# Block 0's plain float32 second products cut from eight feature chunks to four, and its share of the attention steps moved one or two slots later

## The chip, the cores and the metric

The kernel runs on one core of a Trainium2 chip. The metric is the device time of one execution in microseconds (us), from the first to the last instruction of the slowest core (there is only one). A time is the median over runs. The profile comes from one execution that was recorded by the hardware profiler.

## What is computed

```python
# 1. attention in chunks of 32 queries over a window of 16 + 32 + 8 keys and 8 memory keys
scores = (q_c @ k_full.T) / 8
a = exp(scores - max) / (sum + 1e-9)
out_c = a @ v_full
# 2. x = attention output as 3072 tokens x 512
h = x @ w_in                      # 512 -> 2048
y = (h * cos(h)) @ w_out          # 2048 -> 512
# 3. three products, maximum, one product
z = max(y @ w1, y @ w2, y @ w3)   # 512 -> 768
result = z @ w_out2               # 768 -> 512
```

All of it is float32 work. The weights arrive as 64-bit floats and are turned into 32-bit floats on the chip.

## The kernel before

The 3072 tokens go in six blocks of 512 (`j`). In part 2 each block is taken in 16 chunks of 128 features (`f`); one chunk of one block is a **slot**, so there are 96 slots in a row. Block 0 is slots 0 to 15. In slot `s` three things are written into the program:

- `p1(j, f)`: the first product of chunk `f`. Its result `h` goes to a PSUM buffer. From chunk 2 on, block 0 uses the two buffers of `ps_h` in turn, so the product of chunk f writes into the buffer that chunk f-2 used.
- `chain(j, f)`: h times cos(h). In block 0 it is a copy to integers on ScalarE (L429), a subtraction on VectorE (L430), Sin and Square on ScalarE (L433, L434) and a product with `h` on VectorE (L438 or L443), which is the last to read `h`. Its result is `g`.
- `p2`: the second product, two slots behind (`LOOK = 2`), into four PSUM accumulators.

A product is normally made of three matmuls of the type float32r (L392), of a high part and a low part of each operand: high by high, high by low, low by high. So `g` and the weights have to be split: a copy on ScalarE gives the high part (L446 for `g`, L206 for weights), and a subtraction on GpSimd (L447 for `g`; L207 for weights of the first product) or VectorE (L207 for weights of the second product) gives the low part. In block 0, for chunks below `PLAIN`, the second product is instead one matmul of plain float32 (L389; the trace counts two instructions for each), which needs no split of `g`, and the split of that chunk's weight is put off: `split_out` does it from slot `SPLIT0` on, a fixed fraction of a chunk in each slot (`SPLITS`), so that block 1 has it.

In block 0 the engines beside TensorE also decode the weights: per slot one chunk of either weight is loaded, its top bits are taken (L181 on ScalarE, L183 on GpSimd), it is put together (L198 on VectorE), and chunks decoded one slot earlier are split.

Beside all this, block 0 computes the attention of block 1, in four parts `d` of 128 queries. The tables `FIRST` (block 0), `SECOND` (block 1) and `STEADY` say in which slot each step of it stands: `S` scores on TensorE (L246) into the two buffers of `ps_a`, then a sum with the mask and a maximum on VectorE (L263, L269) and a subtraction on GpSimd (L270); `E` Exp on ScalarE for two parts at a time (L274, with a load of ScalarE's function table before it and one back for Sin behind it); `N` the norm (VectorE L279 to L281, GpSimd L282); `T` a transpose on VectorE (L286) and a write to memory; `L` or `l` the three transfers back (`pt`, one buffer; `l` stands behind the `V` before it); `V` the product with v on TensorE (L305), the copy of its result to `x` on ScalarE (L307) and the low part on VectorE (L308). Block 1's first product, in slot 16, reads `x` of all four parts.

The order on each engine is that of the program as the scheduler put it. TensorE's order is pinned throughout, all engines' orders only for the first six slots; an engine takes its instructions strictly in order. All transfers are issued by one queue (SyncE). Parts 3 and the preparation of its weights follow later and are not touched.

Of the kernel before, what the change touches and what calls it, by code (L numbers as in the profile page):

```python
# [46 lines left out]

FIRST = {2: "S0", 3: "S1", 4: "S2", 5: "S3 E01", 6: "E23 N0", 7: "T0 N1", 8: "L0 T1 N2", 9: "V0 l1", 10: "V1 T2 N3", 11: "L2 T3", 12: "V2 l3", 14: "V3"}  # L50
SECOND = {0: "S0", 1: "S1", 2: "E01 S2", 3: "N0 S3", 4: "T0", 5: "E23 N1 L0 S4", 6: "V0 T1", 7: "L1 N2", 8: "S5 T2 N3", 9: "V1 E45", 10: "L2 S6 T3", 11: "V2", 12: "L3 S7", 13: "V3", 14: "E67"}
STEADY = {1: "N0", 2: "T0 N1", 3: "L0", 4: "S4", 5: "V0 T1 N2", 6: "L1", 7: "S5", 8: "V1 T2 N3", 9: "L2 E45", 10: "S6 T3", 11: "V2 l3", 12: "S7", 13: "V3", 14: "E67"}

# [16 lines left out]

PLAIN, SPLIT0, SPLITS = 8, 12, (0.5, 0.75)
INV2PI = 1.0 / (2.0 * math.pi)


# [1 line left out]
def attn_moe_kernel(ctx, tc, qT, kT, vw, w_in, w_out, w3, w2o, out):  # L78
# [141 lines left out]
    def a_load_qk(d):  # L220
        if d >= ND:
            return
        if d < DB:
            q = wp.tile([128, 1024], F32, tag="w", name="q")[:, :2 * 4 * QU].rearrange("p (t h c) -> p t h c", t=2, h=4)
            k = wp.tile([128, 1024], F32, tag="w", name="k")[:, :4 * KD].rearrange("p (h c) -> p h c", h=4)
            live[0] += 2
        else:
            q = t2.tile([128, 2, 4, QU], F32, tag="q", name="q")
            k = t2.tile([128, 4, KD], F32, tag="k", name="k")
        SP.dma_start(out=q, in_=qT[d])  # L230
        SP.dma_start(out=k, in_=kT[d])
        qk[d] = (q, k)
# [16 lines left out]
    def a_scores(d):  # L249
        ss[d] = [ps_a.tile([128, 4, KU], F32, tag="a", name="s") for _ in range(2)]  # L250
        for t in range(2):
            a_s(d, t, ss[d][t], True, keep)
# [4 lines left out]
    def a_add(d):  # L257
        m = sm[d] = t2.tile([128, KB * H * 32], F32, tag="sm", name="sm", bufs=4)
        m = by_key(d)
        p = ss.pop(d)  # L260
        for t in range(2):
            mask = maskb[:, variant(d, t), None, :].to_broadcast([128, 4, KU])
            DVE.tensor_tensor(m[:, 4 * t:4 * t + 4], p[t].rearrange("p h (b k) -> p h b k", b=KB),  # L263
                              mask.rearrange("p h (b k) -> p h b k", b=KB), op=ALU.add)

    def a_max(d):
        m = by_key(d)
        mx = t2.tile([128, H], F32, tag="mx", name="mx")
        DVE.tensor_reduce(mx, m, axis=AX.XY, op=ALU.max)  # L269
        POOL.tensor_tensor(m, m, mx[:, :, None, None].to_broadcast([128, H, KB, 32]), op=ALU.subtract)  # L270

    def a_exp(j, ds):
        for d in (DB * j + i for i in ds):
            keep(ACT.activation(out=sm[d], in_=sm[d], func=AF.Exp, scale=0.125))  # L274

    def a_norm(d):
        m = by_key(d)
        r = t2.tile([128, H], F32, tag="rs", name="rs")
        DVE.tensor_reduce(r, m, axis=AX.XY, op=ALU.add)  # L279
        DVE.tensor_scalar(r, r, 1.0e-9, None, op0=ALU.add)  # L280
        DVE.reciprocal(r, r)  # L281
        POOL.tensor_tensor(m, m, r[:, :, None, None].to_broadcast([128, H, KB, 32]), op=ALU.mult)  # L282
# [6 lines left out]
    def a_l(d):  # L289
        pt[d] = t2.tile([128, 4, H, 32], F32, tag="pt", name="pt", bufs=1)  # L290
        for b in range(KB):
            keep(SP.dma_start(out=pt[d][32 * b:32 * b + 32].rearrange("p a h q -> p a (h q)"),
                              in_=ptd[d % 2][:, 256 * b:256 * b + 256].rearrange("(a p) e -> p a e", a=4)))
# [100 lines left out]
    def p1(j, f):  # L394
        if f % 2 and (done[0] or j == 0 and f == 1):
            h = ps_a.tile([128, N], F32, tag="a", name="h")
        else:
            h = ps_h.tile([128, N], F32, tag="h", name="h")
        w, x = wA_in[f], xT[j]
        for k in range(4):  # L400
            products(h, w, k, [x[:, i, k, :] for i in range(2)], k == 0, k == 3)
        live[0] -= j == NBLK - 1
        hq[j, f] = h
# [4 lines left out]
    def wa_fetch(j, f):  # L408
        if j and f >= RES:
            w = w_tile([128, 2, 512], "wa")  # L410
            SP.dma_start(out=w.rearrange("p a c -> p (a c)").bitcast(F32), in_=wad[f])
            wA_out[f] = (w[:, 0, :], w[:, 1, :])
# [53 lines left out]
    def p2(j, f):  # L466
        g, w = g_t.pop((j, f)), wA_out[f]
        if f == 0:
            acc[j] = [ps_acc.tile([128, N], F32, tag=f"acc{m}", name=f"acc{m}") for m in range(4)]
        for m in range(4):  # L470
            products(acc[j][m], w, m, [g[:, i, :] for i in range(2 if j or f >= PLAIN else 1)], f == 0, f == FA - 1)
        live[0] -= f >= RES or j == NBLK - 1
        if f == FA - 1:
            for m in range(4):
                if m < 3:
                    t = tr.tile([128, N], F32, tag="r", name="x2")
                elif done[0]:
                    t = tmp["pool"].tile([128, N], F32, tag="xo", name="x2", bufs=6)
                else:
                    t = t2.tile([128, N], F32, tag="x2", name="x2", bufs=1)  # L480
                if m % 2 == 0:
                    ACT.activation(out=t, in_=acc[j][m], func=AF.Copy, scale=1.0 if j else -2.0)
                elif j:
                    DVE.tensor_copy(t, acc[j][m])
                else:
                    DVE.tensor_scalar(t, acc[j][m], -2.0, None, op0=ALU.mult)
                SP.dma_start(out=x2d[j][:, m, :], in_=t)
# [57 lines left out]
    def flush():  # L545
        while later:
            out, in_ = later.pop(0)
            keep(SP.dma_start(out=out, in_=in_))
# [61 lines left out]
    def prep_go(upto):  # L610
        while prep_n[0] < min(upto, len(prep)):
            prep[prep_n[0]]()
            prep_n[0] += 1
# [366 lines left out]
    def slot(s):  # L980
        j, f = slots[s]
        plan = {0: FIRST, 1: SECOND}.get(j, STEADY)
        todo = plan.get(f, "").split() if j < NBLK - 1 else []
        base = DB * (j + 1)

        ready = dec.nb
        if s < turn:
            dec.begin(RATE)
        if s < FA:
            parts = int(max(0, s - SPLIT0 + 1) * SPLITS[0])  # L990
        else:
            parts = int((FA - SPLIT0) * SPLITS[0] + (s - FA + 1) * SPLITS[1])

        def fill(where):
            if s < 2:
                if where == "z":
                    dec.split_in(ready)
                    dec.bits()
                    dec.load()
                return  # L1000
            if where == "z":
                prep_go(int(sum(i % FA not in QUIET for i in range(PREP0, s)) * PREPS))
            if s >= turn:
                if where == "z":
                    for fn in early.get(s - total, ()):
                        fn()
                return
            if where == "a0":
                dec.split_in(ready)
            elif where == "a1":  # L1010
                dec.split_out(parts)
            elif where == "d0":
                dec.bits(1)
            elif where == "z":
                dec.bits()
                dec.exp(dec.nb + 2)
                dec.load()

        for op in todo:
            if op[0] == "L" and base + int(op[1:]) < ND:  # L1020
                a_l(base + int(op[1:]))
        while wf[0] < min(s + (3 if s >= turn else 2), total):
            wa_fetch(*slots[wf[0]])
            wf[0] += 1
        flush()
        p1(j, f)
        chain(j, f, fill, [base + int(op[1:]) for op in todo if op[0] == "T" and base + int(op[1:]) < ND])

        def do2():
            while n2[0] <= s - LOOK:  # L1030
                p2(*slots[n2[0]])
                n2[0] += 1

        for op in todo:
            d = base + int(op[1:2])
            if d >= ND:
                continue
            if op[0] == "S":
                do2()
                a_scores(d)  # L1040
                a_add(d)
                a_load_qk(d + 2)
                a_max(d)
            elif op[0] == "E":
                a_exp(j + 1, map(int, op[1:]))
            elif op[0] == "N":
                a_norm(d)
            elif op[0] == "l":
                a_l(d)
            elif op[0] == "V":  # L1050
                do2()
                a_v(d)
                a_load_v(d + 2)
        do2()
# [117 lines left out]
```

## Time and profile before

| | |
|---|---|
| median of 3 runs | 965.54 us (965.42 to 965.87) |
| the profiled execution, its own time | 967.37 us |
| its span, first to last instruction | 965.5 us |
| TensorE busy | 954.3 us (99%) |
| VectorE, ScalarE, GpSimd busy | 613.6, 461.7, 413.1 us |

How to read it: the profile names engines PE (TensorE matmuls), PEld (its weight loads), DVE (VectorE), ACT (ScalarE), POOL (GpSimd) and SP (SyncE). L392 is line 392 of the kernel. In a timeline each row gives the start, the duration, the engine, the line, the operation, the result and operands, and in brackets the time that the engine had stood idle and what ended that. Matmuls overlap, so the time one takes is read from one start to the next.

### The profile page before, as it was taken

To read this page: it belongs to the slowest core of one execution; us is meant where nothing else is said; L and a number is where in the kernel's file an instruction comes from. 1 tells how busy PE (TensorE), PEld (TensorE's weight loads), DVE (VectorE), ACT (ScalarE), POOL (GpSimd) and SP (SyncE) were. 2 spreads that over 40 slices of the span, in tenths; PEclk is the share of its full clock that TensorE was granted. 3 is DMA by queue.
4 is the path that set the end of the run, shared out by engine and by line. 5 is a ranking of instruction groups with operands and counts; after the bars stand their busy time and mean duration, and the time that the engine had idled before them with its cause. 6 is when DMAs were issued, how large, how long until landed. Compare 5 with 4: busy or idle time off the path is not lost.

```text
span 965.5 us, 14586 instructions
## 1 busy us (share of the span) xinstructions
PE 954.3 (99%) x5372; PEld 770.0 (80%) x5373; DVE 613.6 (64%) x923; ACT 461.7 (48%) x801; POOL 413.1 (43%) x333
## 2 busy tenths in 40 slices
PE   8999999999999999999999999999999999999998
PEld 5666788888888888888888888888888888888886
DVE  7688856655667656765646475644784657945565
ACT  6667645555445554564545545523363332723333
POOL 3566535534345445445434355435501545025520
PEclk9999999999999999999999999999999999999999
DMA  9986633563557855775477739695568647595502
GB/s 289 337 306 198 224 126 103 160 197 142 192 198 221 252 196 174 226 227 186 147 216 247 241 113 323 226 319 164 174 229 330 243 135 230 202 390 172 193 23 88
DMA packets 75911, 201.75 MB, mean 209 GB/s; under 512 B 8256, under 2 KB 21056, under 8 KB 75840
## 3 DMA queue, kind: packets, MB, share of 16 engines
q1 hardware_dynamic: 75552, 200.56, 62.2%
q8 instruction: 43, 0.70, 0.3%
q10 hardware_dynamic: 288, 0.26, 0.1%
q14 instruction: 28, 0.23, 0.1%
HBM read 154.13 MB, written 46.66 MB: 208 GB/s over the span
## 4 chain that ended last, share of the span: by engine, by line
PE 93%; DMA 3%; DVE 2%; ACT 1%; issue 1%; SPq 0%; POOL 0%; DVEq 0%; ACTq 0%
PE hb L734 27%; PE h L392 26%; PE acc L392 23%; PE hb L861 9%; PE s L246 3%; PE acc L389 3%; PE s L305 2%; DMA v<-in_vw_dram 1%; DMA k<-in_kT_dram 1%; DMA pt<-ptd 1%; ACT ki L455 0%; DVE ki L453 0%; DVE ki L452 0%; DVE ki L457 0%; PE s L356 0%
## 5 line engine op out<-in xcount | busy, mean ns | idle before, releaser
L392 PE MATMUL h<-x,w 128*128 128x512 f32 x1152 | 283.9, 395 | 0.0
L392 PEld LDWEIGHTS h<-x,w 128*128 128x128 f32 x1152 | 213.1, 188 | 48.7 <-issue 1.4
L462 POOL TENSOR_TENSOR g<-ki,g 128x512 fp32r<-128x512 f32 x80 | 108.5, 1356 | 213.5 <-ACT g L461 187.4
L734 PE MATMUL hb<-x,wq 128*128 128x512 f32 x648 | 155.7, 389 | 0.0
L734 PEld LDWEIGHTS hb<-x,wq 128*128 128x128 f32 x648 | 121.6, 188 | 25.3
L392 PE MATMUL acc<-g,w 128*128 128x512 f32 x576 | 138.3, 389 | 0.0
L392 PEld LDWEIGHTS acc<-g,w 128*128 128x128 f32 x576 | 108.1, 188 | 22.5
L734 PE MATMUL hb<-xo,wq 128*128 128x512 f32 x486 | 119.1, 389 | 0.0
L392 PE MATMUL acc<-g,wa 128*128 128x512 f32 x480 | 115.6, 389 | 0.2 <-POOL g L462 0.2
L455 ACT ACTIVATE ki<-ki,pio 128x512 f32<-128x512 f32 x80 | 58.1, 726 | 108.1 <-DVE ki L453 107.9
L734 PEld LDWEIGHTS hb<-xo,wq 128*128 128x128 f32 x486 | 91.2, 188 | 18.9
L392 PEld LDWEIGHTS acc<-g,wa 128*128 128x128 f32 x480 | 90.0, 188 | 19.3 <-POOL g L462 0.6
L760 POOL TENSOR_TENSOR p<-p,p 128x512 f32<-128x512 f32 x27 | 38.4, 1421 | 144.7 <-ACT p L757 144.7
L452 DVE SCALAR_TENSOR_TENSOR ki<-h,ki 128x512 f32<-128x512 f32 x80 | 54.9, 686 | 68.5 <-ACT ki L450 68.5
L457 DVE TENSOR_TENSOR ki<-h,ki 128x512 f32<-128x512 f32 x80 | 55.2, 690 | 55.0 <-ACT ki L455 55.0
L861 PE MATMUL hb<-g,wo 128*128 128x512 f32 x378 | 86.2, 389 | 0.0
L861 PEld LDWEIGHTS hb<-g,wo 128*128 128x128 f32 x378 | 70.9, 188 | 14.7
L461 ACT ACTIVATE g<-ki 128x512 fp32r<-128x512 f32 x80 | 50.6, 633 | 59.0 <-DVE ki L457 58.9
L450 ACT ACTIVATE ki<-h 128x512 int32<-128x512 f32 x80 | 47.2, 590 | 58.6 <-PE h L392 52.1
L760 DVE TENSOR_TENSOR a<-a,hb 128x512 f32<-128x512 f32 x27 | 18.5, 684 | 72.1 <-PE hb L734 72.1
L553 DVE TENSOR_TENSOR wq<-raw,wq 128x512 fp32r<-128x512 f32 x36 | 44.1, 1244 | 24.6 <-ACT wq L552 24.5
L198 DVE SCALAR_TENSOR_TENSOR raw<-raw,top 128x512 int32<-128x512 int32 x48 | 45.9, 956 | 16.3 <-ACT top L181 16.2
(126 smaller groups left out, 1213.3 us busy)
## 6 DMA issues: line engine op xcount, KB each, us to landing
wq<-wd SPq DMA_DIRECT2D x81, 512.0 KB, 6.5
wa<-wad SPq DMA_DIRECT2D x40, 512.0 KB, 6.0
wo<-wod SPq DMA_DIRECT2D x30, 512.0 KB, 4.5
wd<-wq SPq DMA_DIRECT2D x27, 512.0 KB, 2.9
v<-in_vw_dram SPq DMA_DIRECT2D x24, 384.0 KB, 5.8
raw<-in_w_dram SPq DMA_DIRECT2D x18, 511.8 KB, 5.3
raw<-in_w_in_dram SPq DMA_DIRECT2D x16, 511.8 KB, 10.3
raw<-in_w_out_dram SPq DMA_DIRECT2D x16, 511.8 KB, 10.0
```

The costliest lines, as they stand in the source:

```text
L198: keep(DVE.scalar_tensor_tensor(o, z, 13, top[key], op0=ALU.logical_shift_right, op1=ALU.bitwise_or))
L392: PE.matmul(o, lhsT=w[a][:, sl], rhs=x[b], start=first and n == 0, stop=last and n == 2)
L450: row(ACT.activation(out=ki, in_=h, func=AF.Copy, scale=INV2PI, bias=0.25))
L452: row(DVE.scalar_tensor_tensor(c, h, INV2PI, ki, op0=ALU.mult, op1=ALU.subtract))
L455: row(ACT.activation(out=c, in_=c, func=AF.Sin, scale=2 * math.pi, bias=pio2))
L457: row(DVE.tensor_tensor(c, h, c, op=ALU.mult))
L461: row(ACT.activation(out=g[:, 0, :], in_=c, func=AF.Copy))
L462: row(POOL.tensor_tensor(g[:, 1, :], c, g[:, 0, :].bitcast(F32), op=ALU.subtract))
L553: keep(eng.tensor_tensor(w[:, 1, :], src, w[:, 0, :].bitcast(F32), op=ALU.subtract))
L734: keep(PE.matmul(o, lhsT=w[:, a, 256 * half + 128 * c:256 * half + 128 * c + 128], rhs=x[c][:, b, :], start=first and n == 0, stop=n == 5, ...
L760: keep(eng.tensor_tensor(o, a, b, op=op))
L861: keep(PE.matmul(bk[i][b], lhsT=w[:, s, x, 128 * i:128 * i + 128], rhs=g[:, y, :], start=b not in seen and c == 0 and m == 0, stop=c == 2 ...
```

## The change

```diff
-FIRST = {2: "S0", 3: "S1", 4: "S2", 5: "S3 E01", 6: "E23 N0", 7: "T0 N1", 8: "L0 T1 N2", 9: "V0 l1", 10: "V1 T2 N3", 11: "L2 T3", 12: "V2 l3", 14: "V3"}
+FIRST = {3: "S0", 4: "S1", 5: "S2", 6: "S3 E01", 7: "E23 N0", 8: "T0 N1", 9: "L0 T1 N2", 11: "V0 l1", 12: "V1 T2 N3", 13: "L2 T3", 14: "v2 l3", 15: "v3"}
...
-PLAIN, SPLIT0, SPLITS = 8, 12, (0.5, 0.75)
+PLAIN, SPLIT0, SPLITS = 4, 14, (0.5, 0.75)
...
-            elif op[0] == "V":
-                do2()
+            elif op[0] in "vV":
+                if op[0] == "V":
+                    do2()
                 a_v(d)
                 a_load_v(d + 2)
```

Chunks 4 to 7 of block 0 now have a second product of three float32r matmuls; their `g` is split in their own slot, and their weight is split one slot after it is decoded, like the others'. A `v` puts the product with v between the slot's first and second product, where `V` puts it behind both.

ScalarE, around the Exp of the attention, from a chunk's copy of `h` (`sm` is the attention's tile, `top` the bits of a weight). Before, chunks 5 and 6:

```order
L429 ACTIVATE ki<-h 128x512
L206 ACTIVATE w<-raw 128x512
L433 ACTIVATE ki<-ki 128x512
L434 ACTIVATE ki<-ki 128x512
L181 ACTIVATE top_88<-raw 128x512
L274 ACT_TABLE_LOAD
L274 ACTIVATE sm<-sm 128x768 x2
L429 ACTIVATE ki<-h 128x512
L206 ACTIVATE w<-raw 128x512
L433 ACT_TABLE_LOAD
L433 ACTIVATE ki<-ki 128x512
L434 ACTIVATE ki<-ki 128x512
```

And in the changed kernel from chunk 7's copy of `h` to the table load ahead of chunk 8's Sin:

```order
L429 ACTIVATE ki<-h 128x512
L206 ACTIVATE w<-raw 128x512 x2
L433 ACT_TABLE_LOAD
L433 ACTIVATE ki<-ki 128x512
L434 ACTIVATE ki<-ki 128x512
L429 ACTIVATE ki<-h 128x512
L446 ACTIVATE g<-ki 128x512
L181 ACTIVATE top_88<-raw 128x512
L274 ACT_TABLE_LOAD
L274 ACTIVATE sm<-sm 128x768 x2
L206 ACTIVATE w<-raw 128x512 x2
L433 ACT_TABLE_LOAD
```

Each chunk now has a second copy of weights (L206) ahead of its Sin and a copy of `g` (L446) behind its Square, and the second pair of Exp stands between chunk 8's copy of `h` and its Sin.

ScalarE at the end of block 0, around the last product with v (`x<-s` is the copy of its result). Before:

```order
L429 ACTIVATE ki<-h 128x512
L206 ACTIVATE w<-raw 128x512 x2
L433 ACTIVATE ki<-ki 128x512
L434 ACTIVATE ki<-ki 128x512
L446 ACTIVATE g<-ki 128x512
L307 ACTIVATE x<-s 128x4x128
L429 ACTIVATE ki<-h 128x512
L433 ACTIVATE ki<-ki 128x512
```

And in the changed kernel:

```order
L429 ACTIVATE ki<-h 128x512
L206 ACTIVATE w<-raw 128x512
L433 ACTIVATE ki<-ki 128x512
L434 ACTIVATE ki<-ki 128x512
L206 ACTIVATE w<-wt 128x512
L446 ACTIVATE g<-ki 128x512
L307 ACTIVATE x<-s 128x4x128
L450 ACTIVATE ki<-h 128x512
```

The copy of `x` stood between the chains of chunks 14 and 15; now it is the last thing before block 1's first chain (L450).

## Rows read from the trace of the kernel before

**Rows 1.** The page: busy time, share of the span and instructions of each engine.

```profile
PE 954.3 (99%) x5372; PEld 770.0 (80%) x5373; DVE 613.6 (64%) x923; ACT 461.7 (48%) x801; POOL 413.1 (43%) x333
```

**Rows 2.** Groups by line, PE, whole span: busy, mean ns | idle before, releaser.

```profile
L389 PE MATMUL acc<-g,wt 128*128 128x512 f32 x64 | 28.7, 592 | 0.0
```

**Rows 3.** Timeline of PE in block 0: start, duration, what.

```profile
36.32 3.59 PE L389 MATMUL acc<-g,wt 128*128 128x512 f32 x8
...
64.90 3.02 PE L392 MATMUL h<-x,w 128*128 128x512 f32 x12
...
70.78 3.30 PE L392 MATMUL h<-x,w 128*128 128x512 f32 x12
...
76.95 3.30 PE L392 MATMUL h<-x,w 128*128 128x512 f32 x12
...
83.12 3.30 PE L392 MATMUL h<-x,w 128*128 128x512 f32 x12
...
97.80 1.15 PE L305 MATMUL s<-pt,v 96*64 96x64 f32 x32 [1.20 <-DMA pt<-ptd]
...
101.74 2.88 PE L392 MATMUL acc<-g,w 128*128 128x512 f32 x12
...
107.18 2.88 PE L392 MATMUL acc<-g,w 128*128 128x512 f32 x12
109.99 1.15 PE L305 MATMUL s<-pt,v 96*64 96x64 f32 x32
111.07 3.02 PE L392 MATMUL h<-x,w 128*128 128x512 f32 x12
...
134.37 1.54 PE L246 MATMUL s<-k,q 64*64 64x96 f32 x32
...
141.54 1.54 PE L246 MATMUL s<-k,q 64*64 64x96 f32 x32
```

**Rows 4.** Timeline of ACT in slots 6 to 8.

```profile
67.95 0.60 ACT L429 ACTIVATE ki<-h 128x512 int32<-128x512 f32 x1 [1.63 <-PE h L392]
...
73.72 1.58 ACT L274 ACTIVATE sm<-sm 128x768 f32<-128x768 f32 x2
75.21 0.58 ACT L429 ACTIVATE ki<-h 128x512 int32<-128x512 f32 x1
75.69 0.67 ACT L206 ACTIVATE w<-raw 128x512 fp32r<-128x512 f32 x1
76.37 1.28 ACT L433 ACT_TABLE_LOAD   x1
77.67 0.64 ACT L433 ACTIVATE ki<-ki 128x512 f32<-128x512 f32 x1
78.33 0.63 ACT L434 ACTIVATE ki<-ki 128x512 f32<-128x512 f32 x1
...
85.07 0.62 ACT L446 ACTIVATE g<-ki 128x512 fp32r<-128x512 f32 x1
85.59 0.79 ACT L181 ACTIVATE top<-raw 128x512 f16<-128x512 bf16 x1
```

**Rows 5.** Timeline of DVE in slots 7 and 11.

```profile
79.00 0.69 DVE L438 SCALAR_TENSOR_TENSOR g<-ki,h 128x512 f32<-128x512 f32 x1 [0.33 <-ACT ki L434]
...
103.78 1.81 DVE L207 TENSOR_TENSOR w<-raw,w 128x512 fp32r<-128x512 f32 x1
```

**Rows 6.** Timeline of POOL in slot 11.

```profile
103.73 1.31 POOL L207 TENSOR_TENSOR w<-raw,w 128x512 fp32r<-128x512 f32 x1 [1.76 <-ACT w L206]
```

**Rows 7.** Timeline of ACT in slot 15, the last of block 0.

```profile
126.31 0.60 ACT L429 ACTIVATE ki<-h 128x512 int32<-128x512 f32 x1 [1.96 <-PE h L392]
...
129.72 0.64 ACT L446 ACTIVATE g<-ki 128x512 fp32r<-128x512 f32 x1 [0.23 <-DVE ki L443]
```

**Rows 8.** Tile pt, issues of 91 to 93 us, then of 102 to 104 us: time to landing.

```profile
DMA to landing us min/median/max: 5.3/5.5/5.5
...
DMA to landing us min/median/max: 2.8/2.9/2.9
```

## The prediction

> **What bounds the kernel now.** I read the page first: TensorE is busy for 954.3 of 965.5 us, and no other engine for more than 64% [rows 1]. So the time is TensorE's own work plus its waits, and anything that another engine does earlier or later counts only where TensorE then waits. Next come TensorE's groups by line, which give the work that the change takes away [rows 2], and then TensorE's timeline through block 0, which gives the true spacing (the mean of a group overlaps its neighbours) and the waits [rows 3]. Between the first product and the end of block 0 there is one wait: 1.20 us for the transfer `pt` at 97.80. Last I read ScalarE, VectorE and GpSimd in the same slots, to see how early each delivers [rows 4 to 7]. From block 1 on TensorE has no wait worth removing, so what block 0 gains or loses is what the kernel gains or loses.
>
> **Cheaper second products.** A slot with a plain second product and nothing else takes 76.95 - 70.78 = 6.17 us; one with a float32r product takes 107.18 - 101.74 = 5.44 [rows 3]. The difference, 0.73 us, is for four plain matmuls (two instructions each, 64 in 8 chunks [rows 2]) against twelve. Four chunks change: 4 x 0.73 = **2.92 us less work on TensorE**. The scores and the products with v are the same instructions elsewhere, so they cost TensorE nothing more.
>
> **The old wait.** The 1.20 us at 97.80 belongs to the second `V`, one slot behind the first; `pt` has one buffer, so its load starts when the first is done. It was issued at 91 to 93 us, on a busy queue, and landed 5.3 to 5.5 us after issue; on a quieter one at 102 to 104 us it took 2.8 to 2.9 [rows 8]. In the changed kernel the second and the fourth product with v stand that close (about 5.6 us behind the load's cause, of which issuing takes some 1.4). Each could wait 0 to 1.2 us. In the changed kernel fewer weight loads are left for those slots, so I take a value near the quieter row: **1.20 away and 0.3 back** for both (bounds 0 and 2.4).
>
> **More work on ScalarE before chunk 10.** This is the term that I worry about. In block 0 chunk 10's first product overwrites the PSUM buffer of chunk 8, so it must wait until VectorE's L443 of chunk 8 has read it. In the kernel before the tightest such case is chunk 9's: L438 of chunk 7 ends at 79.69 [rows 5], and the product starts at 83.12 [rows 3], 3.4 us later. Now both sides move.
>
> TensorE first. The first plain product starts at 36.32 and takes 3.03 us, chunk 3's slot begins at 39.35. Three slots with scores and a plain product follow: a float32r slot with scores takes 141.54 - 134.37 = 7.17 [rows 3], plus 0.73, so 7.9 each, and chunk 6 begins near 63.1. One slot of 7.17 and three of 5.44 later, **TensorE wants chunk 10 at 86.6**. Before, the same four slots took 90.86 - 64.90 = 26 us (a product with v and four plain ones lay in them), now 23.5.
>
> ScalarE works through the following, in the order that the scheduler built. Spacings are from start to start [rows 4]: copy of `h` 0.5, one weight copy 0.6, table load 1.3, Sin 0.66, Square 0.63, copy of `g` 0.52, top bits 0.79, two Exp 1.5; VectorE's product 0.65 with its hand-over.
> - Chunk 6's copy comes 3.05 us after its product starts (67.95 against 64.90 [rows 3, 4]), at 66.2. Copy, two weight copies, Sin, Square: 3.0. VectorE's product 0.65, and 0.7 more because its weight subtraction (L207) sits ahead of it and GpSimd holds it up; copy of `g` and top bits 1.3. That makes 71.8.
> - Table load and Exp 2.8; chunk 7's copy, weights, table load back, Sin, Square 4.3; VectorE 0.9; `g` and top bits 1.3: 81.1.
> - Table load and second Exp 2.8; weights 1.2, table load 1.3, Sin 0.66, chunk 9's copy 0.5, Square 0.63: 88.2; VectorE's L443 of chunk 8: **88.8**.
>
> So TensorE waits 88.8 - 86.6 = **2.2 us** there. Its lower bound is 0: 2.2 us out of 22 is one wait that I have counted and that overlaps another. For the upper bound: a weight subtraction on VectorE takes 1.81 us instead of 0.69 when it meets one on GpSimd (103.78 beside 103.73 [rows 5, 6]), and two more such meetings on the path make 4.4. Behind it, chunk 8's second product needs the low part of `g`, which by the same walk comes within 0.3 us of its turn; I take nothing for that.
>
> The Trainium skill, ScalarE: Activation LUTs, section What ACT_TABLE_LOAD costs, states 1.28 us for the load and 1.38 us more for draining the engine. By the page, four changes of table would add 5.5 us to the wait. The trace shows the load (1.28 us, at 76.37) starting 0.01 us behind the end of the copy before it and Sin starting 0.02 us after it [rows 4], so here the drain is not seen.
>
> **The last product with v.** Before, it ended 5.6 us ahead of block 1's first product, which reads its result `x`. Now one second product lies between. From the end of chunk 15's first product, product with v 1.08 (111.07 - 109.99 [rows 3]) and second product 2.9 take TensorE 4.0 us on. But the copy to `x` stands behind all of chunk 15's chain on ScalarE: L446 ends about 4.0 us after the chain's first copy (129.72 + 0.55 - 126.31 [rows 7]), which itself starts 0.2 us late; copy 0.6 and VectorE's low part 0.65 bring it to 5.4. Block 1's second matmul needs the low part and would start at 4.25: a wait of **1.1 us** (bounds 0 and 2). If that product waits for `pt`, the two waits overlap.
>
> **The rest.** The splits of weights 4 to 7 leave block 1 and the end of block 0, where no wait of TensorE is attached to them; that is worth nothing. Weight loads pass the loads of q and k in the queue, a slot earlier: nothing waits for either.
>
> **Sum:** -2.92 - 1.20 + 0.3 + 2.2 + 1.1 = -0.5 us, against the span of 965.5 us of the profiled execution. That execution took 967.37 us by its own clock, 1.83 above the median; I apply the difference to the median: 965.54 - 0.5 = **965.0 us**. A measurement of this kernel tells 0.2%, 1.93 us, from no change, so this is "same".
>
> **Rivals.**
> 1. *No new wait.* ScalarE's extra work hides, as the work before hid with 3.4 us to spare, and both new positions of the products with v are early enough. Then -2.92 remains, or -4.1 with the old wait gone: 961.4 to 962.6 us. For it: 2.2 us is small beside the 22 us of queue on which it rests, and no stage of block 0 now waits for a chain. Against it: TensorE gets 2.5 us faster over just these slots while ScalarE gets two `g` copies and three weight copies more, some 2.8 us. With the wait before chunk 10 gone alone, the gain is already 2.7 us. Chance 0.34.
> 2. *The chains become the bound.* VectorE and GpSimd hold each other up more often than I counted, as GpSimd gets four more subtractions of 1.3 us in the slots where it also does the attention's. Then chunk 10 waits 4.4 us, chunk 8's second product up to 1.5 for the low part of `g`, `x` 1.5 to 2 and `pt` 1.2: -4.1 + 8.6 to 9.1, so up to 970.5 us. It decides from new waits of 6.1 us on (4.1 + 1.93). Chance 0.18.
> 3. *Changes of ScalarE's table cost twice what the load shows* when Exp and Sin alternate more tightly: four times 1.28 again on the same path, 5.1 us, 970.1 us. The rows above speak against it. Chance 0.02. It is what the rule of the Trainium skill that is named above would do.
>
> **How the numbers follow.** My forecast has 0.46; it spans 963.6 to 967.5. Faster by over 0.2% is rival 1, 0.34; slower by over 0.2% is rivals 2 and 3, 0.20. The range reaches into both: below 962.0 lies a third of rival 1 (0.1), above 967.8 most of rivals 2 and 3 that go beyond the edge (0.1). So 962.0 to 967.8. The forecast's own bounds, all waits at their lowest and at their highest, are 961.4 and 970.2.
>
> **What the profile will show.** Plain matmuls (L389): 32 instead of 64, some 14 us. The slots from 6 to 9 at 5.44 us but for the scores. TensorE idle before chunk 10's first product, released by VectorE's L443: about 2 us, and L443 of chunk 8 ending near 89 us. TensorE idle before block 1's first product, released by L307 or L308: about 1 us. The wait for `pt` under 1.2 us. If instead chunk 10 starts at 86 to 87 us, rival 1 holds; if waits for `g` (L447) appear in several slots, rival 2. I am wrong on the main term if the four chunks save less than 2.7 us of TensorE's busy time.

## The result and the profile after

The changed kernel takes **980.16 us** (median of 4 runs, 978.32 to 981.69) against 965.62 us for the kernel before in the same comparison: ratio 1.0141, interval [1.0124, 1.0159]. It is slower by 14.5 us. I had forecast 965.0 us and a range up to 967.8. The profiled execution took 981.69 us by its own clock, its span is 979.9 us.

The page of the changed kernel, busy times and granted clock (one digit for 24.5 us):

```profile
span 979.9 us, 14624 instructions
...
PE 960.4 (98%) x5388; PEld 778.5 (79%) x5389; DVE 618.2 (63%) x925; ACT 463.0 (47%) x805; POOL 416.3 (42%) x335
...
PEclk9999889999999999999999999999999999999999
```

Two things stand there already. TensorE has 6 us *more* to do than in [rows 1], though four chunks have less work now. And the granted clock is lower in the fifth and sixth slices, 98 to 147 us, which is the second half of block 0.

The windows view, one row for block 0 (from its first product to block 1's first product) of each kernel. Columns: the stretch, its length, busy time of PE, PEld, DVE, ACT, POOL with instructions, granted clock, DMA share, GB/s. Before:

```profile
27.92:128.83 100.91, 99.71 (x585) 70.62 (x585) 79.29 (x102) 66.33 (x105) 57.17 (x47) 1.00 0.77 255
```

After:

```profile
27.96:143.19 115.23, 104.98 (x601) 78.97 (x601) 83.76 (x107) 70.93 (x114) 64.43 (x52) 0.93 0.69 228
```

Block 0 is 14.3 us longer. What follows it is the same to 0.04 us: 965.5 - 128.83 = 836.67 before, 979.9 - 143.19 = 836.71 after. So the whole loss lies in these 115 us: TensorE busy 5.3 us longer at a mean clock of 0.93, and idle for 10.2 us instead of 1.2.

The timeline of TensorE in block 0 of the changed kernel (start, duration, what, idle before and its releaser):

```profile
39.91 0.73 PE L392 MATMUL h<-x,w 128*128 128x512 f32 x2
41.82 2.56 PE L392 MATMUL h<-x,w 128*128 128x512 f32 x10 [1.18 <-POOL w L207]
...
77.66 2.88 PE L392 MATMUL h<-x,w 128*128 128x512 f32 x12
...
83.09 2.88 PE L392 MATMUL h<-x,w 128*128 128x512 f32 x12
85.81 2.98 PE L392 MATMUL acc<-g,w 128*128 128x512 f32 x12
90.61 4.62 PE L392 MATMUL h<-x,w 128*128 128x512 f32 x12 [1.82 <-DVE ki L443]
95.08 2.90 PE L392 MATMUL acc<-g,w 128*128 128x512 f32 x12
...
103.34 1.15 PE L305 MATMUL s<-pt,v 96*64 96x64 f32 x32
...
107.28 2.88 PE L392 MATMUL acc<-g,w 128*128 128x512 f32 x12
113.24 1.98 PE L305 MATMUL s<-pt,v 96*64 96x64 f32 x32 [3.09 <-DMA pt<-ptd]
115.15 4.78 PE L392 MATMUL h<-x,w 128*128 128x512 f32 x12
119.76 2.89 PE L392 MATMUL acc<-g,w 128*128 128x512 f32 x12
...
129.24 2.88 PE L392 MATMUL h<-x,w 128*128 128x512 f32 x12
136.29 1.97 PE L305 MATMUL s<-pt,v 96*64 96x64 f32 x32 [4.16 <-DMA pt<-ptd]
138.19 5.16 PE L392 MATMUL acc<-g,w 128*128 128x512 f32 x12
143.19 2.91 PE L392 MATMUL h<-x,w 128*128 128x512 f32 x12
```

I compare each start-to-start spacing with the same stretch undisturbed. Twelve float32r matmuls take 2.72 us (83.09 to 85.81), or 2.86 right behind a product with v; the products with v take 1.08 (together 3.94, 103.34 to 107.28), and one starts 2.81 behind the product ahead of it (107.18 to 109.99 [rows 3]). There are four waits, and three of them have a tail:

| place | wait | more time behind it |
|---|---|---|
| chunk 3's first product, for weights (GpSimd L207) | 1.17 | none |
| chunk 10's first product, for L443 of chunk 8: 4.80 - 2.72 | 2.08 | 4.47 - 2.72 = 1.75 |
| second product with v, for `pt`: 5.96 - 2.81 | 3.15 | 0.83 + 1.75 |
| fourth product with v, for `pt`: 7.05 - 2.81 | 4.24 | 0.82 + 2.14 |
| sum | 10.6 | 7.3 |

The tails are instructions that run longer. The same 32 matmuls of L305 take 1.15 us at 103.34 and 1.98 at 113.24. The windows view of the changed kernel gives the granted clock (first number behind the brackets):

```profile
90.61:95.08 4.47, 4.46 (x13) 3.51 (x14) 4.47 (x4) 2.55 (x5) 4.47 (x4) 0.62 0.23 90
113.24:119.76 6.52, 6.52 (x44) 5.47 (x45) 3.03 (x3) 1.83 (x3) 1.27 (x1) 0.56 0.80 234
136.29:143.19 6.90, 6.90 (x44) 5.75 (x45) 2.45 (x4) 2.80 (x5) 1.28 (x1) 0.53 0.60 209
```

Before each stretch TensorE stood idle for 1.8 to 4.2 us, and the granted clock is between 0.53 and 0.62: mostly the lower of its two levels, 1.2 GHz, and 2.4 for the rest. After the 1.18 us at 41.82, and after the 1.20 us in the kernel before [rows 3], nothing of this is seen.

The account: 10.6 + 7.3 - 2.92 (plain matmuls) - 1.20 (the old wait) = 13.8 of the 14.3 us. The other 0.5 lies ahead of chunk 3 too: its first product starts 3.55 us behind the plain product (36.36 to 39.91), where the prediction has 3.03.

Why is `pt` so late? The timeline of SyncE's queue in the changed kernel:

```profile
105.44 0.34 SPq L169 DMA_DIRECT2D raw<-in_w_in_dram  x1
105.87 0.38 SPq L239 DMA_DIRECT2D v<-in_vw_dram  x1
106.36 1.35 SPq L292 DMA_DIRECT2D pt<-ptd  x3
...
125.13 0.34 SPq L287 DMA_DIRECT2D ptd<-sm  x1
125.51 0.43 SPq L169 DMA_DIRECT2D raw<-in_w_out_dram  x1
126.04 0.41 SPq L548 DMA_DIRECT2D wad<-w  x1
126.55 0.40 SPq L239 DMA_DIRECT2D v<-in_vw_dram  x1
127.82 2.51 SPq L292 DMA_DIRECT2D pt<-ptd  x3
```

The buffer of `pt` comes free when the first product with v ends, at 104.5. But a load of raw weights stands ahead, and by the waits of SyncE it waits until 105.44 for a weight tile, until GpSimd's L207 has ended (us in all, times, longest):

```profile
SPq L169 <- POOL w L207: 4.9, 1, 4.9
```

Then comes `v`, then `pt`, whose three pieces land 5.8 to 6.1 us after their issue. At 127.82 `pt` is again behind raw weights, a write of weights and `v`, and lands after 6.3 to 7.5 us. This time the raw weights do not hold up its issue: the buffer came free at 126.5, `v` went at 126.55, and then SyncE waited 0.7 us for the write of `pt`'s own source, `ptd`, which VectorE's transpose (L286) had let go only at 125.13. So the second `pt` is issued 1.9 us behind the free buffer, the fourth 1.4 us, and both land late. In the kernel before, the last load of raw `w_in` was issued at 86.17 and no raw load stood between the first product with v and the second `pt` at 91.49; behind `v` alone it landed after 5.3 to 5.5 us [rows 8], and the wait was 1.20:

```profile
86.17 0.38 SPq L169 DMA_DIRECT2D raw<-in_w_in_dram  x1
86.60 0.53 SPq L169 DMA_DIRECT2D raw<-in_w_out_dram  x1
...
90.97 0.34 SPq L239 DMA_DIRECT2D v<-in_vw_dram  x1
91.49 1.27 SPq L292 DMA_DIRECT2D pt<-ptd  x3
```

### The profile page after: what moved, and what is told of

The parts are those of the page before. It is cut to its first block, busy times and chain, and to the rows that moved or that the text cites. A ratio compares the mean times of both kernels' runs of the same rounds, so it can differ in the third digit from the quotient of the medians.

```text
span 979.9 us, 14624 instructions
## 1 busy us (share of the span) xinstructions
PE 960.4 (98%) x5388; PEld 778.5 (79%) x5389; DVE 618.2 (63%) x925; ACT 463.0 (47%) x805; POOL 416.3 (42%) x335
## 4 chain that ended last, share of the span: by engine, by line
PE 86%; DMA 4%; DVE 3%; ACT 3%; issue 2%; POOL 1%; SPq 1%; DVEq 0%; ACTq 0%; POOLq 0%
PE hb L734 26%; PE h L392 23%; PE acc L392 22%; PE hb L861 9%; PE s L246 3%; PE s L305 2%; DMA pt<-ptd 1%; DMA v<-in_vw_dram 1%; PE acc L389 1%; DMA k<-in_kT_dram 1%; POOL w L207 1%; DMA ptd<-sm 1%; DVE w L207 0%; ACT ki L455 0%; ACT top L181 0%
## 5 line engine op out<-in xcount | busy, mean ns | idle before, releaser
L392 PEld LDWEIGHTS h<-x,w 128*128 128x128 f32 x1152 | 215.4, 190 | 52.7 <-DVE ki L443 2.2
L392 PE MATMUL acc<-g,w 128*128 128x512 f32 x624 | 152.4, 394 | 0.0
L734 PEld LDWEIGHTS hb<-x,wq 128*128 128x128 f32 x648 | 121.7, 188 | 25.2
L392 PEld LDWEIGHTS acc<-g,w 128*128 128x128 f32 x624 | 118.6, 191 | 25.3 <-POOL g L447 0.2
L450 ACT ACTIVATE ki<-h 128x512 int32<-128x512 f32 x80 | 47.2, 590 | 66.5 <-PE h L392 58.3
L198 DVE SCALAR_TENSOR_TENSOR raw<-raw,top 128x512 int32<-128x512 int32 x52 | 48.7, 939 | 17.3 <-ACT top L181 12.9
L553 DVE TENSOR_TENSOR wq<-raw,wq 128x512 fp32r<-128x512 f32 x36 | 44.1, 1244 | 24.5 <-ACT wq L552 24.5
```

What stands on the lines that cost most here:

```text
L198: keep(DVE.scalar_tensor_tensor(o, z, 13, top[key], op0=ALU.logical_shift_right, op1=ALU.bitwise_or))
L392: PE.matmul(o, lhsT=w[a][:, sl], rhs=x[b], start=first and n == 0, stop=last and n == 2)
L450: row(ACT.activation(out=ki, in_=h, func=AF.Copy, scale=INV2PI, bias=0.25))
L553: keep(eng.tensor_tensor(w[:, 1, :], src, w[:, 0, :].bitcast(F32), op=ALU.subtract))
L734: keep(PE.matmul(o, lhsT=w[:, a, 256 * half + 128 * c:256 * half + 128 * c + 128], rhs=x[c][:, b, :], start=first and n == 0, stop=n == 5, ...
```

## The experiments

In the profiled executions, one of each program, the first product starts anywhere between 25.2 and 31.8 us, and what follows block 0 takes 836 to 838 us, but for `spread6_res7` with 839.2, where TensorE waits 2.5 us for `g` later on. So the ratio to the kernel before carries some microseconds of the start, and the length of block 0 is the finer measure: 100.91 before, 115.23 after. "Block 0" below is this length. The letters in the expectations name the theories of the moment: A lays the loss on the later table, B on the four chunks, C on the clock behind the waits, D on the order of the queue, G on the pool of weight tiles; E and F belong to the repairs.

### Each half alone

`plain4_old_first` has four plain chunks and the old table:

```diff
-FIRST = {3: "S0", 4: "S1", 5: "S2", 6: "S3 E01", 7: "E23 N0", ...
+FIRST = {2: "S0", 3: "S1", 4: "S2", 5: "S3 E01", 6: "E23 N0", ...
```

> The changed kernel with the attention steps of block 0 back in their old slots; four plain chunks stay. Theory A (the moved products with v cause most of the loss, by their late pt): 963 to 968 us, one wait of at most 1.5 us for pt, and a wait of about 2 us for a chain's last reader of h before chunk 9 or 10, with some 2 us of half clock behind it. Theory B (the extra splits of chunks 4 to 7 cause the loss): 976 us or more.

969.32 us, ratio 1.0037 [1.0019, 1.0054], block 0 102.52. The timeline of its TensorE has two waits, the first with a slow product behind it, the second without:

```profile
83.01 4.61 PE L392 MATMUL h<-x,w 128*128 128x512 f32 x12 [2.31 <-DVE ki L443]
...
91.69 1.15 PE L305 MATMUL s<-pt,v 96*64 96x64 f32 x32 [1.32 <-DMA pt<-ptd]
```

`plain8_new_first` has the new table and eight plain chunks:

```diff
-PLAIN, SPLIT0, SPLITS = 4, 14, (0.5, 0.75)
+PLAIN, SPLIT0, SPLITS = 8, 12, (0.5, 0.75)
```

> The kernel before with only the attention steps moved; eight plain chunks stay. Theory A: 974 to 978 us (965.6 and the two pt waits of 3.1 and 4.2 us, less the old 1.2, with 2.6 and 3.0 us of half clock behind them). Theory B: within 1.5 us of 965.6.

968.88 us, 1.0038 [1.0022, 1.0053], block 0 102.95. It waits 1.17 us at chunk 3 and 1.48 us at the fourth product with v, and not at the second.

So neither half makes the loss. They cost 1.6 and 2.0 us of block 0 alone and 14.3 together; theories A and B, which each gave it to one half, both fall. The loss is a meeting of the two. With four plain chunks the raw weights come late (the last `w_in` is loaded at 108.47 with the old table, at 105.44 in the changed kernel, against 86.17 before and 88.46 in `plain8_new_first`), and only the later table has a product with v close behind: with the old one the last `pt`, at 112.34, stands behind raw weights too, but its product comes at 122.89 and does not wait.

### The clock

`fill_waits` keeps every step of the changed kernel, and has TensorE multiply two constants into the PSUM tile of the product with v while `pt` is on its way, 14 and 18 times; the product overwrites them.

```diff
+        if d in FILL:
+            for _ in range(FILL[d]):
+                keep(PE.matmul(..., lhsT=identb, rhs=..., start=True, stop=True))
```

> The changed kernel with 14 and 18 spare matmuls (results overwritten) on TensorE in front of the second and the fourth product with v, so that it is busy while pt is on its way. Theory C (the clock falls to half because TensorE stood idle): the pt waits end at the same moment, the twelve matmuls behind each take 2.9 us again instead of 4.6 and 5.0, and the time is 973 to 976 us. Rival (the clock falls for another reason): the clock is at half there as before, 979 us or more.

Block 0 109.64, 5.6 us shorter. The timeline of TensorE at the two places:

```profile
113.92 2.45 PE L305 MATMUL s<-maskb,identb 128*128 128x384 bf16 x14
116.86 1.15 PE L309 MATMUL s<-pt,v 96*64 96x64 f32 x32 [0.50 <-DMA pt<-ptd]
117.95 3.01 PE L396 MATMUL h<-x,w 128*128 128x512 f32 x12
...
132.99 3.10 PE L305 MATMUL s<-maskb,identb 128*128 128x384 bf16 x18
137.53 1.15 PE L309 MATMUL s<-pt,v 96*64 96x64 f32 x32 [1.44 <-DMA pt<-ptd]
138.61 3.02 PE L396 MATMUL acc<-g,w 128*128 128x512 f32 x12
```

The transfers are as late as before, but the product with v takes 1.15 us and the one behind it 3.0, and the windows view has 1.00 there; the wait before chunk 10, which was not filled, keeps its 0.62:

```profile
94.54:98.98 4.44, 4.44 (x12) 3.49 (x13) 4.44 (x4) 2.53 (x5) 4.44 (x4) 0.62 0.23 90
116.86:120.80 3.94, 3.94 (x45) 3.38 (x45) 2.27 (x2) 0.60 (x1) 1.03 (x1) 1.00 0.83 274
137.53:141.47 3.94, 3.94 (x44) 3.38 (x45) 1.98 (x3) 2.18 (x4) 1.30 (x1) 1.00 0.64 183
```

That is theory C: the tails behind the `pt` waits, 5.5 us in the table above, go when TensorE does not stand idle. The time hardly fell (979.41 us, 1.0133 [1.0109, 1.0156]) and misses the 973 to 976 that C forecast. In the profiled execution the first product starts at 31.83 instead of 27.96, with loads of `v` and `k` late: 31.83 + 109.64 + 836.6 is its span of 978.1. Why the start is late there, no run shows.

### What stands ahead of `pt`

`pt_two` gives parts 1 and 3 a `pt` of their own, from the pool of weight tiles, so that their load waits for no product:

```diff
-FIRST = {..., 11: "V0 l1", 12: "V1 T2 N3", 13: "L2 T3", 14: "v2 l3", 15: "v3"}
+FIRST = {..., 11: "L1 V0", 12: "V1 T2 N3", 13: "L2 T3", 14: "L3 v2", 15: "v3"}
...
+            pt[d] = wp.tile([128, 4, H, 32], F32, tag="w", name="pt")
```

> The changed kernel with a second buffer for pt in parts 1 and 3 of block 0, and their loads issued at the start of slots 11 and 14 instead of behind a product with v. Theory A1 (pt is late because its load is issued late): both waits under 1 us, 966 to 969 us. Rival A2 (pt is late because the transfers ahead of it in the queue take that long whenever it is issued): waits of 2 us or more stay, 974 us or more.

973.78 us, 1.0095 [1.0068, 1.0122], block 0 109.16. The second and fourth products with v no longer wait. The third now does, for 3.88 us with a slow product behind it, and beside the old wait at chunk 3 (1.18) weights come late in two more places (0.66 and 1.52 us), perhaps since `pt` now takes tiles of their pool, which no run separates. So neither theory's time came out. The wait of 1.79 us before chunk 10 has no slow product behind it (3.01 us), where 1.82 us in the changed kernel has one.

`pt_first` keeps one `pt` and issues it ahead of `v` and of raw weights in slots 11 to 14:

```diff
-                dec.load()
+                if s not in (11, 12, 13, 14):
+                    dec.load()
...
-                a_load_v(d + 2)
+                    after_pt.append(d + 2)
+        while after_pt:
+            a_load_v(after_pt.pop())
+        if s in (11, 12, 14):
+            dec.load()
```

> The changed kernel with only the order of its transfers altered in slots 11 to 14: the loads of pt for parts 1 and 3 are issued ahead of the load of v and of the next raw weights. Theory D (pt is late because raw weights, which wait for a free buffer, and v stand ahead of it in the one queue): the two pt waits fall from 3.1 and 4.2 us to about 1 us each, the half clock behind them goes, and the time is 968 to 971 us; the waits before chunks 3 and 10 stay. Rival (the load of pt takes as long wherever it stands): waits of 2.5 us or more, 976 us or more.

973.59 us, 1.0081 [1.0062, 1.0099], block 0 108.08. SyncE's queue behind the first product with v, which ends at 105.0, now starts with `pt`:

```profile
105.00 2.35 SPq L292 DMA_DIRECT2D pt<-ptd  x3
107.39 0.43 SPq L239 DMA_DIRECT2D v<-in_vw_dram  x1
```

Its pieces land after 2.6 to 3.2 us, and the fourth `pt` after 2.2 to 2.9. The timeline of its TensorE at the second, third and fourth products with v:

```profile
110.55 1.15 PE L305 MATMUL s<-pt,v 96*64 96x64 f32 x32
...
123.00 1.98 PE L305 MATMUL s<-pt,v 96*64 96x64 f32 x32 [2.91 <-DMA pt<-ptd]
...
132.62 1.15 PE L305 MATMUL s<-pt,v 96*64 96x64 f32 x32
```

Both waits of the changed kernel are gone by the order of the queue alone, so the raw weights and `v` ahead of `pt` were their cause. In `plain8_new_first`, which has the same table, `v` alone stands ahead of the second `pt`; it lands after 3.9 to 4.1 us, and its product does not wait. Block 0 is only 7.2 us shorter, and the forecast of 968 to 971 us is missed, since a wait of 2.91 us with a slow product behind it is new: the raw weights that were put off now stand ahead of the third `pt`, which also waits 3.3 us for the write of `ptd`. The wait for `x` before block 1, which I had forecast, shows here: 0.41 us (0.42 in `pt_two`).

`after_res6` is the changed kernel with two weight tiles given back to the pool.

```diff
-RES = 8
+RES = 6
```

> The changed kernel, with the second weights of chunks 6 and 7 stored and fetched again in later blocks instead of kept on the chip (10 more of 8), which gives two weight tiles back in block 0. Theory G (the pool of weight tiles is full, so raw weights are loaded late and stand ahead of pt): the last raw first weights are issued before 98 us instead of at 105, the two pt waits fall from 7.2 us together to under 4, and the time is 970 to 976 us. Rival (the decoding is late for another reason): the last raw loads stay at 105 us or later, 978 us or more. If the added fetches cost anything, TensorE waits for them in blocks 1 to 5.

978.49 us, 1.0145 [1.0114, 1.0176], block 0 112.86. The last raw `w_in` is issued at 96.56 instead of 105.44: the full pool did hold the queue. The waits for `pt` fall only from 7.2 to 5.2 us (3.99 and 1.21), as the second is issued at 109.09, 2.7 us later than in the changed kernel: the queue is now held until 107.38 by a write of split weights (9.2 us, for VectorE's L207), and a raw `w_out` at 107.75 and `v` still stand ahead. New waits of 1.56 and 0.65 us for weights come. Theory G explains a part of the lateness, not all.

### Can the four chunks' saving be had?

The wait before chunk 10 (or 9) was attacked with Exp one slot later (`exp_later`), the first Exp also one slot earlier (`exp_wide`), and six plain chunks (`plain6_old_first`), each with the table before as its base (`exp_later` and `plain6_old_first` are shown against `plain4_old_first`, `exp_wide` against `exp_later`):

```diff
-5: "S3 E01", 6: "E23 N0", 7: "T0 N1",
+5: "S3 E01", 6: "N0", 7: "E23 T0 N1",
```

> Four plain chunks and the old slots of the attention, but the second pair of Exp one slot later (7 instead of 6). Theory E (the wait before chunk 9 comes from ScalarE changing tables ahead of chunk 7's Sin): chunk 8's Sin has 1.3 us more room because a product with v lies before chunk 10, the wait and the half clock behind it go (4.2 us less than with the old slots), 963 to 965 us, block 0 some 2.5 us shorter than before the change. Rival (VectorE and GpSimd are the bound, whatever the Exp): a wait of 2 us before chunk 10 or 11, 967 us or more.

```diff
-4: "S2", 5: "S3 E01", 6: "N0",
+4: "S2 E01", 5: "S3", 6: "N0",
```

> As the kernel with the second pair of Exp in slot 7, and the first pair in slot 4 instead of 5. Theory E: the same or a little less waiting than with only the second pair moved, 962 to 965 us. Rival: a new wait in slot 5 or 6, since scores and Exp now meet in slot 4: 966 us or more.

```diff
-PLAIN, SPLIT0, SPLITS = 4, 14, (0.5, 0.75)
+PLAIN, SPLIT0, SPLITS = 6, 13, (0.5, 0.75)
```

> Six plain chunks and the old slots of the attention. Theory F (each plain chunk fewer saves 0.73 us on TensorE as long as the chain of chunk 7 keeps its 3.4 us of room): 1.5 us shorter than before the change, no wait before chunk 9 over 0.5 us, 963.5 to 965 us. Rival (any split of g before the Exp are done costs the wait): a wait of 2 us before chunk 9, 967 us or more.

| | us | ratio | block 0 | waits in block 0 |
|---|---|---|---|---|
| `exp_later` | 968.34 | 1.0018 [0.9997, 1.0038] | 102.73 | `pt` 1.33, 2.54 |
| `exp_wide` | 967.88 | 1.0013 [0.9994, 1.0033] | 102.29 | `pt` 0.22, 2.39 |
| `plain6_old_first` | 969.04 | 1.0030 [1.0020, 1.0041] | 103.6 | L443 0.50, `pt` 2.47 |

The wait for L443 goes when Exp moves, but the 2 us do not: TensorE then comes earlier to a product with v, waits 2.4 to 2.5 us for its `pt`, and runs slowly behind that.

`spread4` sets the products with v two slots apart and loads `pt` ahead of the rest; `spread8` is the same with eight plain chunks, `spread2` with two.

```diff
+FIRST = {2: "S0", 3: "S1", 4: "S2 E01", 5: "S3", 6: "N0", 7: "E23 T0 N1", 8: "L0 T1 N2", 9: "V0 l1", 10: "T2 N3", 11: "v1 l2", 12: "T3 V2 l3", 14: "V3"}
...
+        if s in (9, 11, 12):
+            dec.load()
```

> Four plain chunks; scores in the old slots, Exp in slots 4 and 7, the products with v in slots 9, 11 (between its two products), 12 and 14, each load of pt issued right behind the product with v before it, ahead of the load of v and of raw weights. Theory D with E: no wait over 0.7 us between chunk 0 and block 1, no half clock, block 0 (from the first product to block 1's first) 97 to 99 us against 100.9 before, 962 to 965 us. Rival (with the splits of chunks 4 to 7 the engines beside TensorE are too full in block 0): waits of 2 us or more appear elsewhere, block 0 101 us or more.

> The same attention slots and transfer order with eight plain chunks. If plain chunks cost 0.73 us of TensorE each, block 0 is 2.9 us longer than with four, 99.7 to 101 us: the old wait for pt of 1.2 us is gone and nothing else. If the engines beside TensorE are the bound with four, it is shorter than with four.

> The same attention slots and transfer order with two plain chunks. If nothing waits, block 0 is 1.5 us shorter than with four. If chunks 2 and 3, whose splits meet the decoding of weights at its densest, cannot be hidden, a wait of 1.5 us or more appears before chunk 4, 5 or 6 and block 0 is as long as with four or longer.

Then the same table with more room for weights: `spread4_res6` (`RES = 6`) and `spread6_res7` (six plain chunks, `RES = 7`).

> Four plain chunks, the spread attention slots, and two weight tiles back in the same way. Theory G: the wait of 3.1 us for weights before chunk 15 goes, block 0 is 97 to 99.5 us, 962 to 965 us. Rival (the other engines are too full with four plain chunks): waits of 2 us or more stay, 967 us or more.

> Six plain chunks, the spread attention slots, and one weight tile back. Theory G: no wait over 0.7 us, block 0 97.5 to 99 us, 1.5 us shorter than with eight plain chunks. Rival: as for four plain chunks, a wait of 1 us or more in slots 6 to 15, no gain over eight.

| | us | ratio | block 0 | waits in block 0 |
|---|---|---|---|---|
| `spread8` | 964.96 | 0.9995 [0.9981, 1.0009] | 99.61 | none |
| `spread4` | 973.74 | 1.0073 [1.0056, 1.0090] | 107.29 | `pt` 0.98, 1.17; weights 0.61 before chunk 14, 3.09 and 0.56 before chunk 15 |
| `spread2` | 974.46 | 1.0082 [1.0064, 1.0100] | 109.5 | weights 5.0 and 1.5, L443 1.31, `g` 1.0, `pt` 0.9 |
| `spread4_res6` | 966.99 | 1.0009 [0.9993, 1.0026] | 101.58 | `pt` 1.9, weights 1.6, `g` 0.2 |
| `spread6_res7` | 968.63 | 1.0028 [1.0011, 1.0045] | 102.83 | weights 2.2, `g` 0.84, 0.77 ahead of a product with v |

The windows view of block 0 of `spread8`: TensorE is busy for all of it.

```profile
26.10:125.71 99.61, 99.61 (x586) 70.58 (x585) 76.72 (x102) 66.31 (x105) 60.01 (x47) 1.00 0.76 259
```

The old wait of 1.20 us can be removed, then, and block 0 is 1.3 us shorter than before; the interval of the whole time still holds 1. With four or fewer plain chunks no version gets below 101.58 us: without waits it would be near 96.7 (99.61 - 2.92), and what is saved returns as waits for weights, `pt` or L443. This version is 15 us faster than the changed kernel, and cannot be told from the kernel before.

## Why the prediction was wrong

**The old wait: the step that failed.** It put both loads of `pt` at 0.3 us together, bounded by 0 and 2.4. They cost 7.4 us (3.15 + 4.24). I had seen that the loads stand close behind the product before them, and that they land in 2.9 or 5.5 us [rows 8]. What I took for granted is that they are issued at once, onto a queue with fewer weights in it. In fact they were issued 1.9 and 1.4 us after the buffer came free, the second behind raw weights that had waited for a tile, the fourth behind `v` and the late write of its own source, and they landed after up to 7.5 us. The order of the queue in the changed program shows raw weights and `v` ahead of `pt`; I weighed it as a quieter queue with fewer weight loads. That was false as a count: from the first product with v to the end of block 0 three loads of raw weights are issued (105.44, 114.32, 125.51), against one before (107.53). `pt_first` shows that this order is the cause.

**A term that was missing: the clock.** Every wait was priced at its own length. Behind three of the four the granted clock fell and TensorE's next instructions cost 7.3 us more; `fill_waits` removed the tails at both `pt` waits. Neither a rival nor a bound held this. Rival 2 with all its waits would have stayed at 970.5.

**"The rest" at nothing** was wrong too: the weights that chunk 3 needs came 1.17 us late, with either number of plain chunks, so from the new table.

**Right: the plain products.** The groups of TensorE in the first 200 us of the changed kernel:

```profile
L389 PE MATMUL acc<-g,wt 128*128 128x512 f32 x32 | 14.4, 592 | 0.0
```

32 instead of 64 [rows 2], and a slot of 5.43 us (77.66 to 83.09) for the 6.17 of the plain one. The sign of being wrong that the prediction named, less than 2.7 us saved of TensorE's busy time, came true only in the total, which the slow products raise by 6 us.

**Right in place and size: chunk 10.** I forecast 2.2 us; it waited 2.08. The line of VectorE that releases it:

```profile
89.88 0.68 DVE L443 SCALAR_TENSOR_TENSOR ki<-ki,h 128x512 f32<-128x512 f32 x1
```

L443 of chunk 8 ended at 90.56 rather than at 88.8, and TensorE was ready at 88.53 rather than at 86.6. Both walks start from chunk 6's first product, which began at 64.91 rather than at 63.1, mostly by the delay at chunk 3. From there L443 took 25.65 us (25.7 forecast) and TensorE 23.62 (23.5), so the difference came out by the walk and not by luck. The walk did not have the slow product behind the wait, 1.75 us more.

**Hidden: the wait for `x`.** 1.1 us forecast, none seen. The fourth product with v waited 4.24 us ahead of it and the term vanished in that, as the text allowed; in `pt_first`, with that wait gone, it was 0.41.

**The rivals.** Rival 1 (no new wait) fell. Rival 2 had the right side, but its waits for the low part of `g` are not seen, and the chains made 2 us of waiting among 10.6. Its GpSimd counts in other places: GpSimd's L207 released chunk 3's weights and the raw load that held the queue. Rival 3 fell by the timeline of ScalarE in the changed kernel:

```profile
85.59 1.22 ACT L206 ACTIVATE w<-raw 128x512 fp32r<-128x512 f32 x2
86.83 1.28 ACT L433 ACT_TABLE_LOAD   x1
88.12 0.63 ACT L433 ACTIVATE ki<-ki 128x512 f32<-128x512 f32 x1
```

A change of table takes 1.29 us from start to start (86.83 to 88.12), and the load begins 0.02 us behind the copy. The Trainium skill, ScalarE: Activation LUTs, section What ACT_TABLE_LOAD costs, states 1.28 us for the load and 1.38 us more for a drain. The load agrees with it, and the drain is not seen in these rows.

**What stays open.** How much of the lateness of raw weights is the pool and how much the decoding (`after_res6` moved the last `w_in` by 9 us and won 2.4 us of block 0). How much of the late landing of `pt` is raw weights and how much `v` or writes of weights. And which idle stretches cost the clock: 1.82 us before chunk 10 did and 1.79 us in `pt_two` did not.

## What to carry to other kernels

A transfer can be as late as what stands ahead of it in its queue, and the queue here was held by the first load that had no buffer (4.9 us) or the first write that had no data (9.2 us in `after_res6`); so for each moved load, list what is issued between its cause and itself, and what *that* waits for. Price a wait of TensorE with the work behind it at the lower clock as a second bound: here 10.6 us of waits cost 17.9. Two edits that cost 2 us each can cost 14 together where both use the same slack; run the halves and the whole before either is judged.

## What was not expected of the hardware

- Idle stretches of 2.08, 3.15 and 4.24 us of TensorE, amid work that is dense otherwise, were followed by 1.75, 2.6 and 3.0 us of extra time with the granted clock at 0.53 to 0.62. Spare matmuls on constants in the same gap kept it at 1.00.
- The same three pieces of `pt` took 2.2 to 3.2 us from issue to landing where they were issued first (the second and fourth of `pt_first`), 3.9 to 5.5 right behind `v` alone (`plain8_new_first`, [rows 8]), 5.8 to 6.1 behind 512 KB of raw weights and 384 KB of `v`, and 6.3 to 7.5 in slot 14.
- The first product's start differs by up to 6.6 us between the profiled executions of programs that differ only from block 0 on. With one profile of each, it is not shown whether the program or the execution does it. In `fill_waits` a comparison of totals alone would have read that run as a failure of theory C.
